# Nyström attention plus gated FFN: 96-partition whole-head loads, block-diagonal inverse steps, and attention of the next batch woven between matmul pieces by hand

## Chip, cores, metric

One core of a Trainium2 chip. The metric is the device time in microseconds (us) of one execution; lower is better. Each changed kernel was timed in the same rounds and on the same chip as the kernel before. Engines: TensorE (PE), its weight loads (PEld), VectorE (DVE), ScalarE (ACT), GpSimd (POOL), and SyncE (SP), which here only issues DMAs. A profile's span is 1.8 to 2.0 us shorter than the time. The experiments ran on three chips, on which the kernel before took 496.3 to 498.6 us (medians), so a difference of about 2 us between two changed kernels says nothing.

## The reference, cut to what matters

```python
# q, k, v: (8 batches, 8 heads, 576 tokens, 64); m = 32 landmarks, each the mean of 18 tokens
q_lm, k_lm = q.reshape(B,H,32,18,64).mean(3), k.reshape(B,H,32,18,64).mean(3)
A  = softmax(q    @ k_lm.T / 8)          # 576 x 32
Bm = softmax(q_lm @ k_lm.T / 8)          # 32 x 32
C  = softmax(q_lm @ k.T    / 8)          # 32 x 576
Z  = Bm.T / (norm1(Bm) * norminf(Bm) + 1e-6)
for _ in range(6): Z = 2*Z - Z @ Bm @ Z  # six inverse steps
x  = heads_to_columns(A @ Z @ C @ v)     # 4608 tokens x 512
h  = (x @ w1) * (x @ w2) @ w3            # 4608 x 1024
out = h @ w_out                          # 4608 x 512, float32
```

## The kernel before

Both kernels fold w3 and w_out into one matrix `w34` (the *fold*, in FP32, once), push C·v through w1 and w2 per head (*project*), make both gate inputs from the normalised query scores `ahat` (*up*, eight pieces per batch), and multiply by `w34` (*down*, 36 row chunks of 128 in all). What differs is how query and key arrive, how the six inverse steps are made, and the order.

```python
CH = [(0,128),(128,128),(256,128),(384,128),(512,64)]
def load_attn(b):                              # tokens on partitions, runs of one head: 256 B
    for c, (s0, sz) in enumerate(CH):
        for t, src in enumerate((q, k)):
            nc.gpsimd.dma_start(out=qkn[0:sz, c, t, :]..., in_=src[b, :, s0:s0 + sz, :]...)
    # v: five loads on SP in the same way
def load_weights():                            # w1, w2 to both partition halves, with a cast
    ... nc.gpsimd.dma_start(out=wdup[64*i:64*i+64, :, t, :], in_=w.rearrange("(h d) j -> d h j", d=D))
def attention(b, st):
    for c, (s0, sz) in enumerate(CH): nc.sync.dma_start_transpose(out=qkT[..., s0:s0+sz], in_=qkn[0:sz, c])
    for t in (1, 0): nc.vector.reduce_sum(out=lm[:, t], in_=qkT[:, t] ...)      # landmarks
    # ... cut: scores, the start of Z, C·v
    for it in range(6):                        # inverse steps: eight 32x32 products each
        psI = small()
        for qd in range(2):
            for h in range(4):
                nc.tensor.matmul(psI[sl, ...], sz_[sl, qd, 0:32], sz_[sl, qd, ...],
                                 tile_position=(32*h, 32*h))
        nc.vector.tensor_copy(out=nsz[:, :, 0:32], in_=pv_[:, :, 0:32])
        nc.vector.tensor_tensor(out=nsz[:, :, 32:96], in0=sz_[:, :, 32:96], in1=pv_[:, :, 32:96], op=ALU.add)
    # ... cut: zt, denominators, ahat
load(0); load_weights(); load(1)
attention(0, sts[0]); fold(pf); attention(1, sts[1])
for b in range(B):
    if b + 2 < B: load(b + 2)
    if b > 0 and b + 1 < B: attention(b + 1, sts[b + 1])
    project(sts[b]); up(sts[b], ab, ...); down(ab, ...)
```

The softmax here doesn't subtract the row's maximum and nothing guards it: scores larger than these inputs give would overflow.

## Time and profile before

| | before |
|---|---|
| time, median | 497.8 us (495.1 to 500.2, 4 runs) |
| first PE instruction | 70.9 us |
| first up piece | 205.4 us |
| steady cost of a batch | about 42.5 us |
| mean granted PE clock | 0.859 |

The page of the kernel before: busy us by engine, then 40 equal slices of the span (12.4 us each) with the busy share in tenths; PEclk is the granted PE clock.

```profile
span 497.7 us, 7829 instructions
PE 330.3 (66%) x3264; PEld 188.7 (38%) x3264; DVE 200.4 (40%) x423; ACT 109.2 (22%) x189; POOL 80.7 (16%) x114
PE   0000026056999973896698588669858859967996
PEclk9999999998999985795698589579759967956999
DMA  9999999999221059229936992901760200200112
```

The PEclk line shows two regimes: nothing on PE for five slices while DMA is at 9, and then, from the fifteenth slice on, dips of the clock that come back with every batch. The windows table of the same kernel gives numbers to that: us, busy us of each engine with its instruction count, then the granted clock, DMA share, GB/s. The last three rows are most of one batch: the attention chain with the projection, up, down; the first 6.6 us of its attention (221.4 to 228) are not in them.

```profile
core 0: us, PE busy (x) PEld busy (x) DVE busy (x) ACT busy (x) POOL busy (x), PEclk, DMA share, GB/s
0.00:70.90 70.90, 0.00 (x0) 0.00 (x0) 11.16 (x42) 1.28 (x1) 20.72 (x32) 1.00 1.37 187
228.00:246.00 18.00, 11.32 (x152) 6.20 (x149) 9.44 (x21) 2.27 (x3) 6.32 (x9) 0.51 1.04 133
246.00:257.00 11.00, 9.23 (x67) 6.42 (x67) 9.81 (x11) 4.94 (x9) 2.30 (x4) 1.00 0.95 60
257.00:265.00 8.00, 8.00 (x39) 3.51 (x37) 0.76 (x1) 2.73 (x5) 0.00 (x0) 1.00 0.25 98
```

In 18 of the 42.5 us of a batch PE runs at half clock and has work for 11 us only. (The trace has no clock record before 109 us, so the 1.00 of the first row, and the nines before that in the PEclk line, are not measured. The 16 products of one inverse step at 79.3 us took 0.86 us, as they do later at half clock.) The chain of waits shows why: start, us, and what ran. One inverse step follows another, PE then DVE then PE, 1.49 us each.

```profile
229.87 0.90 PE small L251 x16
230.76 0.02 issue
230.79 0.23 DVE sz__1303 L258
231.01 0.20 DVE sz__1303 L259
231.22 0.14 issue
231.35 0.90 PE small L251 x16
```

For the start, the list of waits names the landmark reduce and what it waited for (us in total, times, longest):

```profile
DVE lm L134 <- DMA qkT<-qkn: 74.6, 4, 58.2
```

Why the transposes took so long stands in the DMA records of the trace, counted here by packet size in a 2 us stretch of the kernel before:

```
from 44 us, 2 us, weights and transposes under way: 177 packets of 2048 B (172 ns each), 179 packets of 256 B (31 ns each)
from 96 us, 2 us, transposes alone:                  1515 packets of 256 B (21 ns each)
```

The 2048 B packets are the weights (4096 B read, cast to half), the 256 B ones transposes. They go through one for one, in number. So a transpose moves at the pace of the weights, about 90 packets per us instead of about 760. The Trainium skill, "DMA: Bandwidth & Descriptors", section "Queues, rings and completion order", says that each engine takes turns between its queues packet by packet; this trace agrees in the counts (it does not name a packet's engine), and shows the price when one queue's packets are 172 ns and the other's 31.

### The profile page before, as it was taken

To read this page: it belongs to the slowest core of one execution; us is meant where nothing else is said; L and a number is where in the kernel's file an instruction comes from. 1 tells how busy PE (TensorE), PEld (TensorE's weight loads), DVE (VectorE), ACT (ScalarE), POOL (GpSimd) and SP (SyncE) were. 2 spreads that over 40 slices of the span, in tenths; PEclk is the share of its full clock that TensorE was granted. 3 is DMA by queue.
4 is the path that set the end of the run, shared out by engine and by line. 5 is a ranking of instruction groups with operands and counts; after the bars stand their busy time and mean duration, and the time that the engine had idled before them with its cause. 6 is when DMAs were issued, how large, how long until landed. Compare 5 with 4: busy or idle time off the path is not lost.

```text
span 497.7 us, 7829 instructions
## 1 busy us (share of the span) xinstructions
PE 330.3 (66%) x3264; PEld 188.7 (38%) x3264; DVE 200.4 (40%) x423; ACT 109.2 (22%) x189; POOL 80.7 (16%) x114
## 2 busy tenths in 40 slices
PE   0000026056999973896698588669858859967996
PEld 0000014033445442454354344435435435544552
DVE  4000062165111136733763393285349346235460
ACT  0000010000000120440243045034305404412452
POOL 6231207066000006000600240000000000000000
PEclk9999999998999985795698589579759967956999
DMA  9999999999221059229936992901760200200112
GB/s 253 185 179 205 169 74 133 168 148 175 91 69 42 1 96 173 18 86 174 95 40 160 127 86 89 185 5 42 140 117 1 86 1 2 100 8 1 43 43 107
DMA packets 160179, 48.75 MB, mean 98 GB/s; under 512 B 151440, under 2 KB 151440, under 8 KB 160144
## 3 DMA queue, kind: packets, MB, share of 16 engines
q0 software_dynamic: 77120, 13.64, 35.0%
q1 hardware_dynamic: 80832, 28.32, 29.2%
q10 hardware_dynamic: 2192, 6.29, 3.7%
q8 instruction: 26, 0.43, 0.4%
q14 instruction: 9, 0.07, 0.1%
HBM read 42.99 MB, written 9.44 MB: 105 GB/s over the span
## 4 chain that ended last, share of the span: by engine, by line
PE 56%; DMA 15%; DVE 13%; issue 5%; ACT 4%; SPq 3%; POOL 3%; POOLq 0%; ACTq 0%; DVEq 0%
PE small L347 13%; PE big L333 13%; PE small L371 11%; DMA qkn<-in_k_dram 11%; PE small L251 6%; PE big L313 4%; SPq L127 3%; PE small L218 3%; POOL qkn L104 3%; DMA qkT<-qkn 2%; DMA qkn<-in_q_dram 2%; PE small L268 2%; PE big L298 2%; ACT a_sb L338 2%; DVE lm L134 2%
## 5 line engine op out<-in xcount | busy, mean ns | idle before, releaser
L333 PE MATMUL big<-ahat,gt 128*128 128x288 f16 x512 | 73.1, 286 | 8.9 <-ACT a_sb L338 5.8
L134 DVE TENSOR_REDUCE lm<-qkT 128x128 f16<-128x2304 f16 x16 | 40.6, 2543 | 74.6 <-DMA qkT<-qkn 74.6
L347 PE MATMUL small<-w_131,ab 128*128 128x512 f16 x288 | 65.3, 379 | 0.0
L333 PEld LDWEIGHTS <-gt 128*128 128x128 f16 x512 | 49.1, 97 | 35.5 <-issue 15.6
L371 PE MATMUL small<-wof,w3t 128*128 128x512 f32 x128 | 59.0, 616 | 3.9 <-DVE w3t L368 3.9
L339 DVE TENSOR_TENSOR ab<-a_sb,big 128x576 f16<-128x576 f16 x64 | 47.5, 753 | 17.8 <-ACT a_sb L338 16.1
L338 ACT CAST a_sb<-big 128x576 f16<-128x576 f32 x64 | 40.9, 639 | 39.9 <-PE big L333 39.9
L151 PE MATMUL small<-lm,qbd 128*64 128x32 f16 x32 | 2.0, 197 | 71.0 <-DVE qbd L140 71.0
L104 POOL DMA_DIRECT2D qkn<-in_q_dram x40 | 35.3, 882 | 66.3 <-DMA qkT<-qkn 46.5
L180 POOL TENSOR_TENSOR bmn<-bm,rn 128x64 f32<-128x64 f32 x8 | 2.6, 326 | 255.6 <-DVE rn L175 255.6
L347 PEld LDWEIGHTS <-ab 128*128 128x128 f16 x288 | 27.8, 98 | 32.6 <-DVE ab L339 1.8
L371 PEld LDWEIGHTS small<-wof,w3t 128*128 128x128 f32 x128 | 24.7, 198 | 34.4 <-issue 29.1
L104 POOL DMA_DIRECT2D qkn<-in_k_dram x40 | 35.1, 877 | 15.0 <-DMA wdup<-in_moe_w_dram 9.2
L350 ACT ACTIVATE o_sb<-small 128x512 f32<-128x512 f32 x36 | 21.5, 597 | 43.4 <-PE small L347 43.4
L298 PE MATMUL big<-rmix,selc 128*128 128x144 f16 x64 | 8.9, 319 | 33.3 <-DVE rmix L292 33.3
L151 PEld LDWEIGHTS <-qbd 128*64 128x64 f16 x32 | 1.2, 112 | 74.3 <-DVE qbd L140 71.0
L368 DVE COPY w3t<-big 128x512 f32<-128x512 f32 x16 | 10.6, 688 | 42.2 <-PE big L364 29.4
L274 ACT ACTIVATE zt<-small 128x256 f16<-128x256 f32 x8 | 3.1, 384 | 110.0 <-PE small L268 110.0
L313 PE MATMUL big<-wdup,zt 128*32 128x512 f16 x256 | 26.1, 578 | 0.3 <-ACT gt L319 0.3
L319 ACT ACTIVATE gt<-big 128x1024 f16<-128x1024 f32 x16 | 16.3, 1024 | 35.7 <-PE big L313 35.7
L321 DVE TENSOR_SCALAR gt<-big 128x1024 f16<-128x1024 f32 x16 | 19.2, 1220 | 10.5 <-PE big L313 10.4
L159 DVE TENSOR_REDUCE rbs<-ebm 128x2 f32<-128x64 f32 x8 | 1.8, 220 | 52.8 <-ACT ebm L156 52.8
(260 smaller groups left out, 321.1 us busy)
## 6 DMA issues: line engine op xcount, KB each, us to landing
out_dram<-o_sb SPq DMA_DIRECT2D x36, 256.0 KB, 2.0
vt<-in_v_dram SPq DMA_DIRECT2D x32, 256.0 KB, 5.4
w3f<-in_moe_w_dram ACTq DMA_DIRECT2D x8, 512.0 KB, 4.7
qkn<-in_q_dram POOLq DMA_DIRECT2D x32, 128.0 KB, 6.6
qkn<-in_k_dram POOLq DMA_DIRECT2D x32, 128.0 KB, 7.2
wdup<-in_moe_w_dram POOLq DMA_DIRECT2D x4, 1024.0 KB, 23.8
wof<-in_moe_w_out_dram ACTq DMA_DIRECT2D x1, 2048.0 KB, 11.0
vt<-in_v_dram SPq DMA_DIRECT2D x8, 128.0 KB, 6.4
```

Of the source, the lines that this page charges most:

```text
L104: nc.gpsimd.dma_start(out=qkn[0:sz, c, t, :].rearrange("p (h d) -> p h d", d=D), in_=src[b, :, s0:s0 + sz, :].rearrange("h p d -> p h d"),)
L134: nc.vector.reduce_sum(out=lm[:, t, :, :], in_=qkT[:, t, :, :].rearrange("p r (l g) -> p r l g", g=GRP), axis=AX.X,)
L251: nc.tensor.matmul(psI[sl, 96 * qd + (32 if last else 0):96 * qd + 96], sz_[sl, qd, 0:32], sz_[sl, qd, (32 if last else 0):96], start=True ...
L298: nc.tensor.matmul(psD[:, c // 2, QS * (c % 2):QS * (c % 2) + QS], selc[:, qd, c, :], rmix[:, :], start=True, stop=True)
L313: nc.tensor.matmul(psG[32 * h:32 * h + 32, n, :], st["zt"][:, 4 * qd + h, :], wdup[:, 4 * qd + h, w, 512 * n:512 * n + 512], start=True, s ...
L321: nc.vector.tensor_scalar(out=dst, in0=psG, scalar1=1.0 / ZS, scalar2=None, op0=ALU.mult)
L333: nc.tensor.matmul(p[:, c, 0:HS], st["g"][qd][:, w, 128 * j:128 * j + 128], st["ahat"][qd][:, c, :], start=(qd == 0), stop=(qd == 1))
L338: nc.scalar.copy(out=a_sb, in_=ps[0][:, :, 0:HS])
L339: nc.vector.tensor_tensor(out=ab[:, j, off:off + S].rearrange("p (c s) -> p c s", c=2), in0=a_sb, in1=ps[1][:, :, 0:HS], op=ALU.mult)
L347: nc.tensor.matmul(pso[:, :], ab[:, j, 128 * t:128 * t + 128], w34[:, j, :], start=(j == 0), stop=(j == 7))
L350: nc.scalar.activation(out=o_sb, in_=pso[:, :], func=AXF.Copy, scale=1.0 / (X64 * X64))
L371: nc.tensor.matmul(psW[:, :], w3t[:, c4, :], wof[:, c, :], start=(c == 0), stop=(c == 7))
```

## The change

Intent: (1) put 96 partitions with 6 consecutive tokens each, so that a query or key load is one DMA with runs of 1536 B; (2) make an inverse step from two 128-wide block-diagonal products instead of eight 32x32 ones; (3) fix the program order by hand: attention becomes a generator whose stages are laid between the up and down pieces of the batch before it, and the fold starts at once, with attention 0 laid into it.

```diff
-            for t, src in enumerate((q, k)):                      # five chunks each
-                nc.gpsimd.dma_start(out=qkn[0:sz, c, t, :]..., in_=src[b, :, s0:s0 + sz, :]...)
+        for t, src in ((1, k), (0, q)):
+            nc.gpsimd.dma_start(out=qkn[0:NP, t, :, :],
+                                in_=src[b].rearrange("h (p r) d -> p h (r d)", p=NP))   # NP = 96
 ... four transposes a batch (t, half of the heads) instead of five; landmarks as 16 small
 ... reduces and one FP32 product; the columns of the scores now come as (c, g, s):
+            nc.scalar.activation(out=e.rearrange("p (s g c) -> p c g s", g=3, c=2),
+                in_=psA[:, :, 0:HS].rearrange("p c (g s) -> p c g s", g=3), func=AXF.Exp, ...)
 ... a softmax row sum of C as six partial sums per head on DVE:
+            nc.vector.reduce_sum(out=es[0:NP], in_=ects[qd][0:NP].rearrange("p h r m -> p h m r"), axis=AX.X)
 ... inverse steps
-                for h in range(4):
-                    nc.tensor.matmul(psI[sl, ...], sz_[sl, qd, 0:32], sz_[sl, qd, ...], tile_position=(32*h, 32*h))
+                nc.tensor.matmul(psI[:, 96*qd+o:96*qd+96], rbd[:, qd, :, :]..., sz_[:, qd, o:96], ...)
+                nc.vector.tensor_tensor(out=nrbd, in0=pv_[:, :, 0:32]..., in1=mask4..., op=ALU.mult)
-                nc.vector.tensor_copy(out=nsz[:, :, 0:32], in_=pv_[:, :, 0:32])
+                if it < 4: nc.scalar.copy(out=nsz[:, :, 0:32], in_=pv_[:, :, 0:32])
 ... the start, and the loop
+    load_qk(sts[0], 0); fd = fold(pf); next(fd); load_v(sts[0], 0)   # fold: w3 on SP, 3 buffers
+    pre = prepare(0); next(pre)                                      # transposes of batch 0, on SP
+    load_weight(0, moe_w1); load_weight(1, moe_w2); load_qk(sts[1], 1); load_v(sts[1], 1)
+    ... 28 fold steps, the last 8 with landmarks, then fold and attention(0) in turn
+        for j in range(8):
+            up(st, j)
+            next(at, None)                                           # a stage of attention b+1
+        ...
+                down(srcs, r, half, hold, bank)
+                next(at, None); next(pre, None)                      # and of the landmarks of b+2
```

## The prediction

> **What bounds it now.** The page and the chain of waits show two parts. (1) Start, 0 to 202 us. TensorE (PE) does nothing before 70.9 us while DMA is over 90% busy; landmark reduces wait 58.2 us for transposes. The DMA records show why: while the weights load (34 to 56 us), engines alternate one 2048 B weight packet (172 ns) with one 256 B transpose packet, 88 transpose packets per us; alone about 700 pass. The FP32 fold starts only at 105.8 us and takes 63 us of PE (64 products of two passes of 0.437 us, 64 transposes of 0.109); attention 1 follows. (2) Steady, 42.5 us per batch. Windows table of batch 1: up 8.5 us and down 7 to 8.7 at granted clock 1.00; but 18 us (228 to 246) at 0.51, a serial chain of small products and VectorE (DVE) steps (iterations of 1.49 us, 0.86 of it PE). The Trainium skill, "TensorE: Matmul & The Clock Gate", Part 1, says an idle PE falls to half clock; this trace agrees (0.50).
>
> **What the change does.** Attention b+1 is woven between up and down pieces, so the clock should stay at 1.00 and chain waits hide. Loads become 1536 B runs (12288 query/key packets instead of 73728). The fold starts before attention 0. Transposes stay 4608 packets a batch.
>
> **Steady, per batch, at full clock (estimates from traced durations).**
> PE: up 8.6, down 7.8 (+0.4 split chunk), projection 2.0, FP32 landmark sum 0.87 (new), key scores 1.7, query scores 0.7, C·V 2.4, iterations 3.0 (from psZ's 1.19 us cold), rest 2: about 29.
> DVE: ab 5.8, 16 landmark reduces 6.5 (was 5.1), block-diagonal masks 2.2 (new), presums 1.7 (new), qbd 0.6, gt 2.4, ahat 1.5, reciprocal chain 1.7, small ones 6: about 28.5. ACT about 15.
> PE and DVE nearly balance. Up phase PE-bound, about 15.7 us; down phase DVE-bound, about 18.5 (landmarks, the reciprocal holding the single small bank, gt evictions before the next up). About 34 against 42.5.
>
> **Start.** SP carries w3, w_out, v, transposes and the remaining w3 loads in one order. w3 blocks 0, 1 and w_out land by 15 us, so the fold begins near 7 us. But w3 block 2 stands behind transposes 0 and v 1, and those transposes share engines with the weights: 2048 packet pairs of 181 ns over 16 engines, 23 us. Key transposes land near 46 us, query near 56, block 2 near 60. PE stalls from about 22 to 60 after 3 of 16 half blocks. Then 51 us fold, 12.6 attention 0, 6 stalls: first up at about 130 us (was 206).
>
> **Total:** 130 + 7×34 + last batch 8.6 + 8.7 + tail 3.2 = 388. Predicted 388 us, range 360 to 415; chances: faster 0.97, within 2% 0.02, slower 0.01.
>
> **What would show the steps.** Granted clock near 1.0 from 65 us on; batches 33 to 35 us apart; iterations off the chain; DVE total 230 to 240 us; PE idle about 35 us in the start, released by the third w3 load; PE busy below 300 us.
>
> **What would make it wrong.** If the transposes are not starved, block 2 lands near 30 us and the start is 100: 360. If in-order DVE waits spread (a multiply behind an attention step, then a PSUM bank, then PE), batches cost 38: 415. If strided XY reduces or the interleaved exponent write run slower than one element per cycle, DVE grows several us per batch. If PE gaps in the down phase still drop the clock, most of the steady gain goes.

## The result, and the profile after

414.83 us median (412.99 to 415.42, 4 runs) against 497.78: ratio 0.833, 95% interval 0.827 to 0.838. A ratio is the mean time of one kernel's fast runs over that of the other's in the same rounds, so not quite the ratio of the medians. The time lies in the predicted range, but only by 0.2 us, with two of the four runs above 415, and 27 us above the point: that it is inside is luck.

The same lines of the page, for the changed kernel (slices of 10.3 us):

```profile
span 413.4 us, 7393 instructions
PE 308.5 (75%) x3056; PEld 173.9 (42%) x3056; DVE 242.9 (59%) x562; ACT 141.2 (34%) x213; POOL 24.3 (6%) x42
PE   3830005998999978787897778789678868887896
PEclk9995556999999999999999999999959999999999
```

The clock now stays at 9 from the eighth slice on but for one slice. PE works from 4.4 us, stops for three whole slices, and is then at 6 to 9 tenths but for the slice in which it starts again. The windows table of the changed kernel, with the columns of the table of before: two parts of the start, the rest of the fold with attention 0, then the up and the down stage of one batch.

```profile
0.00:25.00 25.00, 16.27 (x40) 7.20 (x40) 8.96 (x46) 1.87 (x2) 6.68 (x14) 1.00 1.03 245
25.00:66.00 41.00, 0.01 (x1) 0.00 (x0) 0.00 (x0) 0.00 (x0) 0.00 (x0) 0.55 1.18 193
66.00:136.00 70.00, 66.71 (x411) 33.22 (x412) 36.63 (x83) 13.94 (x21) 2.59 (x4) 0.97 0.60 102
172.30:187.50 15.20, 12.90 (x236) 8.95 (x234) 12.32 (x27) 10.45 (x13) 2.60 (x4) 1.00 1.17 190
187.50:209.30 21.80, 17.85 (x133) 8.87 (x134) 15.76 (x37) 6.66 (x13) 0.00 (x0) 1.00 0.28 77
```

So the steady loop keeps clock 1.00, and 41 us of the start are empty on every compute engine. The list of waits names what ended that:

```profile
PE big L434 <- DMA w3f<-in_moe_w_dram: 45.6, 2, 41.2
```

| | before | after | predicted |
|---|---|---|---|
| first up piece (from the timeline) | 205.4 us | 135.1 us | 130 |
| from it to the first up of the last batch | | 256.5 us = 7 x 36.6 | 7 x 34 |
| from there to the end | | 21.8 us | 20.5 |
| time | 497.8 us | 414.8 us | 388 |

Where the 84 us of span went: attention 1 took 25 us before the first projection in the kernel before (177 to 202) and is in the loop now. With that set aside, the start is 205.4 - 25 - 135.1 = 45 us shorter and the rest (292.3 + 25) - 278.3 = 39 us shorter.

The chain of waits in a down stage of the changed kernel answers to the chain shown of before. The step is still on it, with more parts:

```profile
194.31 0.34 DVE rbd L334
194.66 0.02 issue
194.68 0.02 ACTq L339
194.69 0.04 issue
194.74 0.22 ACT sz__1540 L339
194.96 0.02 issue
194.98 0.29 DVE sz__1540 L340
195.27 0.72 DVE parts L143 x2
195.99 0.66 DVE ahat L317
196.65 0.35 DVE rbd L334
```

The mask (`rbd`) on DVE, then the copy on ScalarE, then the add on DVE: one after the other, then landmark reduces, `ahat`, and the next mask. Mask and copy both only read, and read the same columns of one PSUM bank, so the copy need not wait for the mask's values, and yet it starts 0.08 us after the mask's end. The trace has the copy released by the mask in all four steps of this batch that have a copy. The Trainium skill, "PSUM — Partial Sum Buffer", section "PSUM bank collisions raise a hardware error", says that two engines must not touch the same bank and partitions at once and that software keeps them apart; the order seen here fits that.

Two groups of instructions had sizes that I had not foreseen. From the groups by line, first of the kernel before, then of the changed one (count, busy us, mean ns, idle before):

```profile
L241 ACT ACTIVATE eat<-big 128x576 f16<-128x576 f32 x16 | 9.4, 640 | 0.0
```

```profile
L244 ACT ACTIVATE eat<-big 128x576 f16<-128x576 f32 x16 | 33.8, 2133 | 1.7 <-PE big L238 0.8
L202 DVE TENSOR_REDUCE es<-ect 96x128 f32<-96x768 f32 x16 | 23.9, 1495 | 0.0
```

The exponent writes as many elements as before and takes 3.3 times as long, since each half-precision value now goes 12 bytes from the last. The partial sum reads 768 values 128 bytes apart at 1.95 ns each. The Trainium skill, "SBUF — State Buffer", section "Door 1: The DMA port swizzle", says that an access which moves to another 16-byte line pays a penalty; both durations fit it. For the write e3 shows that the order is the cause; for the read no run does.

### The profile page after: what moved, and what is told of

Read it like the earlier page. It is cut to its first block, busy times and chain, and to the rows that moved or that the text cites. A ratio compares the mean times of both kernels' runs of the same rounds, so it can differ in the third digit from the quotient of the medians.

```text
span 413.4 us, 7393 instructions
## 1 busy us (share of the span) xinstructions
PE 308.5 (75%) x3056; PEld 173.9 (42%) x3056; DVE 242.9 (59%) x562; ACT 141.2 (34%) x213; POOL 24.3 (6%) x42
## 3 DMA queue, kind: packets, MB, share of 16 engines
q0 software_dynamic: 14656, 13.63, 22.9%
## 4 chain that ended last, share of the span: by engine, by line
PE 44%; DVE 22%; SPq 10%; issue 9%; ACT 8%; DMA 5%; POOL 0%; ACTq 0%; POOLq 0%
PE acc L457 11%; SPq L88 10%; PE acc L410 10%; PE big L391 6%; PE small L328 6%; DVE ab L398 4%; DVE gt L381 3%; DMA qkn<-in_k_dram 3%; PE big L374 3%; DMA w3f<-in_moe_w_dram 3%; ACT a_sb L397 3%; DVE parts L143 2%; DVE rbd L334 2%; DVE rr L303 2%; DVE ahat L317 2%
## 5 line engine op out<-in xcount | busy, mean ns | idle before, releaser
L391 PE MATMUL big<-ahat,gt 128*128 128x288 f16 x512 | 78.8, 286 | 10.2 <-DVE gt L381 6.7
L410 PE MATMUL acc<-w_79,ab 128*128 128x512 f16 (+1 forms) x304 | 71.6, 388 | 2.3 <-ACT o_sb L416 2.3
L457 PE MATMUL acc<-wof,w3t 128*128 128x512 f32 x128 | 64.8, 632 | 5.3 <-DVE w3t L438 2.4
L143 DVE TENSOR_REDUCE parts<-qkT 128x32 f32<-128x288 f16 x128 | 50.2, 444 | 0.2
L410 PEld LDWEIGHTS <-ab 128*128 128x128 f16 (+1 forms) x320 | 28.2, 105 | 32.5 <-issue 13.8
L457 PEld LDWEIGHTS acc<-wof,w3t 128*128 128x128 f32 x128 | 23.3, 201 | 28.4 <-issue 19.4
L244 ACT ACTIVATE eat<-big 128x576 f16<-128x576 f32 x16 | 33.8, 2133 | 1.7 <-PE big L238 0.8
L416 ACT ACTIVATE o_sb<-acc 128x512 f32<-128x512 f32 x34 | 20.3, 598 | 26.7 <-PE acc L410 26.5
L334 DVE TENSOR_TENSOR rbd<-small,mask_120 128x256 f32<-128x256 f32 x40 | 16.9, 422 | 12.2 <-PE small L328 11.0
L202 DVE TENSOR_REDUCE es<-ect 96x128 f32<-96x768 f32 x16 | 23.9, 1495 | 0.0
L274 PE MATMUL small<-vt,ect 96*32 96x64 f32 x768 | 14.0, 221 | 4.1 <-DVE sz__2330 L283 0.6
## 6 DMA issues: line engine op xcount, KB each, us to landing
wof<-in_moe_w_out_dram SPq DMA_DIRECT2D x8, 256.0 KB, 10.3
```

Source lines behind the costliest of these rows:

```text
L143: nc.vector.tensor_reduce(out=st["parts"][:, t, h, :], in_=st["qkT"][:, t, h, :, :].rearrange("p c (l g) -> p l c g", g=3), axis=AX.XY, op ...
L244: nc.scalar.activation(out=e.rearrange("p (s g c) -> p c g s", g=3, c=2), in_=psA[:, :, 0:HS].rearrange("p c (g s) -> p c g s", g=3), func ...
L334: nc.vector.tensor_tensor(out=nrbd, in0=pv_[:, :, 0:32].unsqueeze(2).to_broadcast([128, 2, 4, 32]), in1=mask4.unsqueeze(1).to_broadcast([1 ...
L391: nc.tensor.matmul(p[:, c, 0:HS], st["g"][qd][:, w, 128 * j:128 * j + 128], st["ahat"][qd][:, c, :], start=(qd == 0), stop=(qd == 1))
L410: nc.tensor.matmul(pso[o:o + sz, :], ab[:, j, s0:s0 + sz], w34[:, j, :], start=(j == 0), stop=(j == 7), tile_position=(0, o))
L457: nc.tensor.matmul(psW[:, :], cur[:, c4, :], wof[:, c, :], start=(c == 0), stop=(c == 7))
```

## Experiments

Eleven kernels, all correct, all timed in three rounds against the kernel before. "After" is the changed kernel, and edits are against it. Times to compare: after 414.8 us, batches 35.5 us (even, four down chunks) and 37.0 us (odd, five), from one landmark product to the next.

### e1: weights behind the transposes

```diff
+        gate = consts.tile([128, 1], FP16, name="gate")
+        nc.gpsimd.tensor_copy(out=gate, in_=sts[0]["qkT"][:, 0, 7, 2, NP - 1:NP])
         load_weight(0, moe_w1)
```

> Edit: the four weight loads (w1, w2) are issued only after the last transpose of batch 0 has landed (a one-column copy on GpSimd of that transpose's result stands before them). Theory A (transposes of batch 0 are starved: engines alternate 172 ns weight packets with 31 ns transpose packets, and w3 block 2 stands behind them in SP's order): transposes then pass at several hundred packets per us, query transposes land by about 28 us instead of about 57, block 2 by about 33 instead of 66, PE idles about 8 us instead of 41, first up at about 103 instead of 136; time 415 - 33 = about 382. Rival B (96-row transposes are slow in themselves, about 10 us each on SP): no earlier landing, time 410 to 418. Weights must land before the first projection (about 55 us against 75 needed).

388.07 us, ratio 0.779 (0.774 to 0.785); 27 us faster than after. The DMA records show 2007 transpose packets in the 2 us from 24 us (about 1000 per us) where after passed 90 per us, and the gate opened at 29.6 us. Windows table of e1: the gap and what follows.

```profile
25.00:39.40 14.40, 0.81 (x2) 0.00 (x0) 0.00 (x0) 0.00 (x0) 4.37 (x7) 0.64 1.03 233
39.40:109.00 69.60, 66.46 (x412) 33.09 (x412) 36.65 (x83) 13.96 (x21) 2.58 (x4) 0.98 0.98 171
```

The gap shrank from 41 to 14 us, the first up came at 108.1 us, and batches stayed at 35.5 and 37.0. Rival B falls: 96-row transposes are quick when nothing stands between their packets. I had expected block 2 of w3 at 33 us; it came at 39.5, because v of batch 1 stood before it on SP and the weights, let go at 29.6, shared the engines with both.

### e2: two more w3 blocks before the transposes

```diff
-            w3f[j] = pf.tile([128, DF], FP32, name="w3f", bufs=3)
+            w3f[j] = pf.tile([128, DF], FP32, name="w3f", bufs=4)
+        for j in range(2, 4): load_w3(j)          # at the end of the first loads, before v and the transposes
```

> Edit: w3 blocks 2 and 3 are issued on SP before the transposes (four buffers instead of three), weights as they are. Theory A: PE goes on with block 2 but now stops at the landmark reduces, which still wait for the starved key transposes (about 45 to 50 us), then for the query ones (about 60); the 41 us gap shrinks to about 20 and the time falls by about 20, to about 395. Rival C (only the place of block 2 in SP's order matters, not the starvation): the gap goes altogether and the time falls by 35 or more, to 380 or less.

401.02 us, ratio 0.806 (0.802 to 0.811); 14 us faster than after. PE went on to 36 us and stopped again. The list of waits of e2:

```profile
DVE parts L143 <- DMA qkT<-qkn: 26.8, 3, 19.2
```

So rival C falls too: with block 2 there, the starved transposes themselves hold the landmark reduces, and DVE, in order, holds the fold's copies. Both facts were needed for the 41 us: the weights starve the transposes, and block 2 stands behind them.

### e3: exponent written in order

```diff
-                out=e.rearrange("p (s g c) -> p c g s", g=3, c=2), in_=psA[...]rearrange("p c (g s) -> p c g s", g=3)
+                out=e.rearrange("p (c s) -> p c s", c=2), in_=psA[:, :, 0:HS]
-            nc.sync.dma_start(out=out[row:row + 128, :], in_=o_sb)
+            # two stores per 128 rows, to out[...].rearrange("(s r) f -> r s f", r=6)[2*g + c, s0:s0+n, :]
```

> Edit: the exponent of the query scores is written in order instead of six-way interleaved (2133 ns each after, 640 before the change); rows are put back in order by the output stores (two strided stores per 128 rows), so the result is right. Theory D (the interleaved write holds ScalarE, so a_sb comes late, a PSUM bank is freed late, and PE waits about 1.7 and 1.2 us in each up phase): write back to about 0.65 us, up phase 16.5 to about 14.5 us, time 415 - 7 x 2.2 = about 400. Rival E (those waits are really DVE's: the partial sums of 1.5 us stand before the multiply; ScalarE had slack): time falls by 5 or less.

407.26 us, ratio 0.819 (0.814 to 0.824). The write fell to 650 ns, but batches only to 34.8 and 36.2: 0.7 us each, not 2.2. Neither theory D nor E alone: the wait is partly ScalarE's.

### e4: partial sums on GpSimd

```diff
-            nc.vector.reduce_sum(out=es[0:NP], in_=... "p h r m -> p h m r", axis=AX.X)
+            # half = e6[:, :, 0:3] + e6[:, :, 3:6];  es = half[0] + half[1];  es += half[2]   (nc.gpsimd)
```

> Edit: the partial sums over six tokens (1495 ns each on DVE, I had estimated 0.86) are made by three adds on idle GpSimd. Theory E (DVE's 1.5 us in front of two multiplies of each up phase holds PE): up phase shorter by 1 to 2 us, time about 405. Theory D (ScalarE's interleaved write is what holds it): time within 3 us of 415. DVE busy falls by about 24 us either way.

409.09 us, ratio 0.823 (0.819 to 0.827). DVE lost 20 us of work (242.9 to 223.1), yet batches stayed at 35.5 and 36.9. The 6 us come from elsewhere, 5 of them from one batch: in after it took 40.5 us where 35.5 was due, and in e4 none did. More on that gap below.

### e5: no weave

```diff
+        drain(at)                                  # attention b+1 to its end, before the up pieces of b
         for j in range(8):
             up(st, j)
-            next(at, None)
```

> Edit: in the steady loop attention of b+1 is run to its end before the up pieces of b; all instructions, loads and the start are those of the changed kernel. If the weave is what gives the steady gain (chain hidden and clock kept): the granted clock falls to 0.5 again in each chain, a batch costs about 47 us instead of 36.5, time about 135 + 7 x 47 + 22 = 485, PE busy above 330 us. Rival (loads and block-diagonal steps carry the gain): below 440.

520.74 us, ratio 1.049 (1.041 to 1.056): slower than the kernel before. A batch costs 51.9 us, more than the 47 I expected. Windows table of e5, one batch: attention, up, down.

```profile
186.70:219.00 32.30, 20.11 (x260) 14.27 (x260) 16.36 (x39) 10.18 (x14) 2.60 (x4) 0.58 0.77 119
219.00:228.00 9.00, 8.86 (x68) 6.20 (x69) 6.37 (x9) 5.10 (x8) 0.00 (x0) 1.00 0.01 2
228.00:239.30 11.30, 8.51 (x44) 3.63 (x39) 6.00 (x17) 2.39 (x4) 0.00 (x0) 1.00 0.25 93
```

The clock is back at 0.58 in the chain, and the new attention takes 32 us when it stands alone. The weave is worth about 15 us a batch, all of the steady gain and more; the other parts of the new attention cost time, and only the weave hides that. PE busy rises from 308.5 to 357.5 us with the same instructions: that is the clock. The chain of waits of e5 gives one inverse step of the new form when nothing is woven into it:

```profile
207.01 1.18 PE small L328 x4
209.32 1.18 PE small L328 x4
```

That is 2.3 us from step to step, where the kernel before took 1.49, both at half clock. So the block-diagonal step, built with its mask and its copy on ScalarE, is slower in a lone chain too.

### e6: inverse steps as before, still woven

```diff
-                nc.tensor.matmul(psI[:, 96*qd+o:96*qd+96], rbd[...], sz_[:, qd, o:96], ...)
-                nc.vector.tensor_tensor(out=nrbd, ..., in1=mask4...)
-                if it < 4: nc.scalar.copy(out=nsz[:, :, 0:32], in_=pv_[:, :, 0:32])
+                # eight 32x32 products, tile_position=(32*h, 32*h)
+                nc.vector.tensor_copy(out=nsz[:, :, 0:32], in_=pv_[:, :, 0:32])
```

> Edit: the inverse steps go back to eight 32x32 products each, no block-diagonal weights, the small copy back on DVE; woven as in the changed kernel. My theory (the down phase is bound by DVE and by the chain product, mask, copy, add; the block-diagonal form moves work from PE to DVE and gains nothing when woven): time within 2% of 415, more likely lower by 3 to 8 (DVE falls by about 10 us, an iteration's chain by about 0.4 us). Rival (block-diagonal steps are part of the gain): slower by 10 or more.

401.93 us, ratio 0.810 (0.804 to 0.816); 13 us faster than after, more than I expected. Batches 33.6 and 35.2. The chain of waits of e6 in a down stage:

```profile
191.16 0.46 PE small L327 x16
191.62 0.97 PE acc L404 x4
192.59 0.25 PE big L311 x4
192.84 0.46 PE small L327 x16
```

Now the chain is PE alone: step, half a down chunk, step. One step takes 0.46 us of PE in sixteen small instructions against 0.69 in four wide ones. The block-diagonal form was slower on PE and put a 0.42 us mask on DVE.

### e7: short runs in the new layout

```diff
-            nc.gpsimd.dma_start(out=qkn[0:NP, t, :, :], in_=src[b].rearrange("h (p r) d -> p h (r d)", p=NP))
+            for r in range(6):                      # 256 B runs, six loads
+                nc.gpsimd.dma_start(out=qkn[0:NP, t, :, 64*r:64*r+64], in_=...[r])
```

> Edit: the same 96-partition layout, but each query/key load is cut into six loads of 256 B runs, as short as before the change. If the long runs carry a gain: the first loads land later (9216 packets a batch instead of 1536, 12 GpSimd issues of about 0.8 us a batch instead of 2), start later by 5 to 15 us, time 420 to 430. If only the start's order matters: within 1% of 415, steady batches unchanged, since DMA is under 30% busy there.

414.52 us, ratio 0.834 (0.826 to 0.841): no difference in the time. In the traces its first up came 1.8 us later (136.9) and its long batch (see below) was 3 us shorter than that of after; the batch after that was 0.7 us longer, the others are alike. The long runs halve the loading queue's DMA time (44.4% of the span in e7, 22.9% in after), but little waited for that time: the start waits for w3, and the loop's loads come two batches early. (DMA is not under 30% busy in the loop, as I had written: its share is 0.53 from 136 to 390 us of after.)

### e8: e3 and e4 together

> Edit: e3 and e4 together (exponent written in order, partial sums on GpSimd). Alone they gave 0.7 and 0.1 us per batch. If the two waits stand in parallel in the up phase (each hides the other's removal): together clearly more than the sum, up phase about 14.5 us, batches 34.8/36.2 become about 33.5/35, time about 397. If they only add: about 403 to 407.

400.00 us, ratio 0.805 (0.798 to 0.811). Batches 33.8 and 35.2, 1.7 us less than after, where e3 and e4 alone gave 0.7 and 0.1. The two waits stand in parallel in front of the same multiply: the exponent makes `a_sb` (ScalarE's copy of one gate input) late on ScalarE, the sum makes DVE late, and taking one away leaves the other.

### e9: block-diagonal steps, the copy on DVE

```diff
-                    nc.scalar.copy(out=nsz[:, :, 0:32], in_=pv_[:, :, 0:32])
+                    nc.vector.tensor_copy(out=nsz[:, :, 0:32], in_=pv_[:, :, 0:32])
```

> Edit: block-diagonal steps as in the changed kernel, but the small copy of each step is on DVE instead of ScalarE. e6 gained 1.9 us per batch by undoing the steps. Theory F (the handoff mask on DVE, copy on ScalarE, add on DVE, which the trace shows one after the other with about 0.3 us of DVE idle, is the larger part): time lower by 6 to 10, about 406. Theory G (the mask itself, 0.42 us on DVE, against a 0.22 us copy before, is what costs): time within 3 of 415.

404.84 us, ratio 0.815 (0.808 to 0.821). One line moved to the busier engine gave 10 us. In the trace about 7 of them are batches of 34.5 and 36.0 us, 1.0 us less each; 2.4 us are a shorter long batch (see below), and 0.9 us the start. Theory F is right that the handoff DVE, ScalarE, DVE costs, but it is about half of what e6 gained (1.9 us a batch), not most of it; the mask and the wider products, which no run separates, are the rest. The chain of waits of e9 shows mask, copy and add without a gap:

```profile
191.95 0.34 DVE rbd L334
192.29 0.13 DVE sz__1540 L339
192.42 0.19 DVE sz__1540 L340
192.61 0.72 DVE parts L143 x2
```

### e10 and e11: all of it

e10 is e1, e2, e3, e4 and e6 in one kernel; e11 is the same with the partial sums left on DVE.

> Edit: e1, e2, e3, e4 and e6 together. Start: blocks 2 and 3 stand before the transposes and the weights after them, so PE should have no gap over 5 us after 8 us: first up at about 98 us (136 in the changed kernel). Batches about 32.5. 98 + 7 x 32.5 + 22 = about 348; if start and steady gains do not add, 355 to 365.

> Edit: as e10 but the partial sums stay on DVE. If they only cost when the interleaved write is gone: 5 to 10 us slower than e10; if they never cost: the same within 2.

e10: 344.19 us (343.96 to 345.04), ratio 0.694 (0.687 to 0.700), the fastest here. First up at 91.6 us, batches 32.8 us on average. Its page:

```profile
span 342.2 us, 8657 instructions
PE 298.6 (87%) x3632; PEld 161.7 (47%) x3632; DVE 206.2 (60%) x538; ACT 113.3 (33%) x181; POOL 54.4 (16%) x91
PE   3899898999997979798979788988889799979994
PEclk9999999999999999999999999999999999999999
```

PE is at 87% and never loses its clock. e11: 351.91 us, ratio 0.709 (0.703 to 0.715), 7.7 us slower than e10. Some 4.4 us of that are not the sums' own work: e11 has the long batch (37.0 us where 32.6 was due) and e10 has not. The other batches are 0.6 us longer (32.6 and 34.1 against 32.0 and 33.5), so the sums do cost once the interleaved write is gone, but little.

### Left open: one long batch

One interval was 1.9 to 4.9 us longer than its like (4.9 in after) in after, e1, e2, e3, e6, e7, e9 and e11, and none was in e4, e8 and e10, the three with the sums on GpSimd, though PE's program is the same in after and e4. The clock records divide the runs in the same way: in each of the eight the clock fell to 0.50 in that batch for 6.8 to 10.2 us, and in the other three it never fell in the loop.

In six of the eight PE also stood still there, with nothing in the profile to wait for: in after for 2.79 us from 298.0 us, in the first inverse step of one batch; in e1, e2, e3, e6 and e11 for 1.5 to 2.4 us. In after a 16384 B packet of the instruction queue starts at 298.0 us, as PE stops, and lasts 1.4 us; in all six the stop ends 1.3 to 1.6 us after the end of such a packet. A late fetch of instructions would look so, but most of the 24 such packets of after pass without a stop, and no run tests it. In e7 and e9, whose batches are 1.9 and 2.5 us longer, the clock fell without such a stop. In after it fell at 298.6 us, only 0.6 us after the stop had begun; in the 3.4 us before, PE had been busy for 1.48. So the stop is not needed for the fall of the clock, and the cause of both stays open.

## Why the prediction was right, and what in it was wrong

- **The direction and the two causes of the gain: right.** The start was predicted to shrink and the chain to be hidden at full clock. e5 shows the second directly. For the first, no run puts the old order of the start back: that the fold starts at 4.4 us, where it started at 105.8 before, stands in the traces, and e1 and e2 show only what still held the new start.
- **"Key transposes land near 46 us, query near 56, block 2 near 60. PE stalls from about 22 to 60": right in mechanism.** After shows 90 transpose packets per us beside the weights, PE idle from 25 to 66 us, released by the third w3 load. The term was 6 us too small: the path behind the transposes (v of batch 1, then block 2) took 11 us, where I had reckoned 4. e1 and e2 show that both the starving and the place in SP's order are needed. First up 135.1, predicted 130.
- **"About 34 against 42.5": the term that was mis-sized.** It is 256.5 / 7 = 36.6, so 7 x 2.64 = 18.5 us of the 27. About 5 of them are the one long batch, whose cause stays open; without it a batch takes (256.5 - 4.9) / 7 = 35.9 us, and 13.6 us are left that the sizes below account for. Three were wrong. The inverse steps: I added mask, copy and add as work on DVE and called the steps "off the chain"; they are on it, because the copy on ScalarE stands between mask and add (e9: 1.0 us a batch; with the old steps, e6: 1.9). The partial sums: I wrote "presums 1.7" us per batch, they are 3.0. The exponent's interleaved write: named only as a danger, it came true at 2133 ns. Exponent and sums together cost 1.7 us a batch (e8), but only taking both away shows it. These savings exceed the 13.6 us (1.9 us a batch) when added, so they overlap or go below what I had predicted; e10, with all of them, is at 32.6 us a batch from first up to first up.
- **"PE and DVE nearly balance": right in a batch** (172.3 to 209.3 us: PE 30.7 and DVE 28.1, I wrote 29 and 28.5). DVE in all was 242.9 us, just over my 230 to 240, and "PE busy below 300 us" was wrong (308.5); the wide inverse steps cost 0.69 us of PE where I had 0.5.
- **"If PE gaps in the down phase still drop the clock": did not happen** in the loop, but for the one long batch.
- **The loads: a neutral part.** I counted 12288 packets for 73728 and gave that no time; e7 agrees.
- **The block-diagonal steps: I did not predict their sign.** They cost 13 us in the woven kernel, and a lone step is slower too (e5: 2.3 us against 1.49).

The remainder (388 to 414.8): 5.1 us start, 18.5 us loop (5 of them the long batch), 1.3 us last batch, 0.5 us of rounding (my terms add up to 388.5), and 1.4 us because I predicted the span and the time is longer.

## What to carry to other kernels

Before you make an operation cheaper, ask what runs beside it once the order changes: in the woven chain what counted was the time of a whole step, with its handoffs from engine to engine, and not the number of products, so fewer and wider products were a loss, and one copy moved back to the busier engine gave 1.0 us a batch. And time one piece of a change alone before you build on it: the new inverse step was slower by itself as well. In a start that is bound by DMA, look at which queue each packet stands in: a small transfer that everything waits for should neither share engines with big packets nor stand in front of the next block of another stream. And when two waits end at the same instruction, taking one away shows little; take both before you call either free.

## What the Trainium skill lacked or had wrong

- "DMA: Bandwidth & Descriptors" (section "Queues, rings and completion order") gives the turn-taking, with a typical packet of about 9 to 17 descriptors, but not what it does to a stream of small packets beside one of large ones: one 256 B transpose packet per 2048 B weight packet, 90 per us, against about 760 to 1000 per us alone.
- "SBUF — State Buffer" (section "Door 1: The DMA port swizzle") names the penalty for leaving a 16-byte line without a size: here a ScalarE write of half-precision values 12 bytes apart took 3.7 ns per element against 1.1 in order, and a DVE read 128 bytes apart 1.95 ns per element. No run changed the read's order on DVE alone.
- "PSUM — Partial Sum Buffer" (section "PSUM bank collisions raise a hardware error") has the rule but not its price: with two readers of one bank on two engines, the second started 0.08 us after the first had ended, and putting both on one engine gave 1.0 us a batch.
- "TensorE: Matmul & The Clock Gate" (Part 1) gives the half clock after an idle window of about 3.4 us, but no share of busy time below which it falls. In after it fell at 298.6 us, after 3.4 us in which PE was busy for 1.48. It came back at 308.9 us, after the first stretch of 3.4 us in which PE was busy throughout (the two before: 1.26 and 2.24 us), which fits the page.
- No page has the 2.79 us stop of PE with nothing to wait for; "Runtime: NRT & Kernel Launch" (section "Instruction fetch mechanics") calls the cost of a fetch mostly hidden. The stop ended 1.4 us after the end of a 16384 B packet of the instruction queue, but these runs do not settle whether it was one.
